# Attention with hash buckets and a mixture of experts on one core: another order for the opening, other gates for the experts' subtractions

## The chip, the cores and the metric

The kernel runs on one core of one Trainium2 chip. The metric is the time of one execution on the device in microseconds (us), the median of several runs. A core has five engines that each run their own list of instructions in order: PE (TensorE, matrix products into PSUM), DVE (VectorE), ACT (ScalarE), POOL (GpSimd) and SP (SyncE, which here only issues transfers). Semaphores order them against each other; 16 DMA engines carry the transfers.

## The reference, cut to what matters

```python
# attention: q, k, v are [4, 8, 768, 64], proj is [64, 6]
q_bits = einsum(q, proj) > 0            # 6 hash bits for each row of q, and of k
mask   = q_bucket[:, None] == k_bucket  # only rows of the same bucket see each other
scores = where(mask, q @ k.T / 8, -1e9)
attn   = exp(scores - max) / (sum + 1e-9)
x      = (attn @ v) as [3072, 512]      # 4 x 768 tokens, 8 heads x 64
# experts: w_gate [512, 8], w1 [8, 512, 1024], w2 [8, 1024, 512], room for 384 tokens each
# greedy choice over the sorted logits x @ w_gate; every token goes to one expert
out[token] = relu(x[token] @ w1[e]) @ w2[e]
```

## The kernel before, in words

**Attention, up to about 425 us.** The 32 heads come in 8 groups of four. For a group the kernel loads q, k and v (`qp`, `kp`, `vp`, 768 KB each, one buffer each) and splits each number into a half-precision part and a remainder: ACT casts (`qh`, `kh`), POOL subtracts (`ql`, `kl`). PE takes the hash bits by a product with `proj`, DVE turns them into signs (`bt`). SP then copies everything into four operands that hold a head's q or k side by side: `qa`, `ka` (rounded parts and hash bits, heads on the second axis) and `qb`, `kb` (rounded parts with the remainders). There are two of each, for odd and even groups (`qa_164` and `qa_168` are the two in the order of before). Group 0 is built piece by piece: heads 0 and 1 straight from loads into `XT`, heads 2 and 3 (its second pair) through `qh`, `kh` and transfers.

A head is worked in 6 steps. In the score pass (`S_pass`, lines 219 and 221) PE forms 128x770 products of `qa` and `ka` and DVE takes their row maxima. In a step (`ST`, lines 243 to 245) PE forms transposed scores, 384 columns at a time, ACT takes the exponential into `pt`; `lo` (line 248, on POOL or DVE) is the remainder of the rounded `pt`; four steps later PE multiplies with `v` (lines 258 to 260). `attention` writes this order out by hand: step t runs `run(2*t)` and `run(2*t+1)`, and the list `at` says what else is emitted at each n = 2t or 2t+1. The table `AP` gives these places: `P1` for group 1's casts, subtractions, hash bits and loads, `MV` for its transfers (`moves`), `OPS` for the whole opening before and during the first steps (one letter an operation: b hash bits of head 0, B those of heads 1 to 3, s score pass, t and r casts into the operands, c and u cast and remainder of the second pair, d and f its transfers, C copies into the other operands' rows 64 to 127, w idle products that keep PE busy). Score passes run up to 9 steps ahead, so that group 1's first one (head 4) stands in PE's list at step 15.

An engine takes its list in order, and SP too: a transfer whose source isn't ready holds up all behind it. Each transfer from SP also waits until the eighth transfer before it has landed.

**Experts, from about 425 us.** `Moe.phase` p chooses the tokens of one expert on DVE with small products on PE (`best`, `compare`, counts, thresholds). `Moe.run` interleaves: while PE works on expert k (`layer1`, 32 pieces, then `layer2`, 36 pieces, 68 in all), the phase of expert k+1 proceeds in steps at the places `E1`, `E2` or `EV`. `wsplit` casts a quarter of a weight on ACT and puts its two subtractions of 128x512 (`wl`, POOL) on a list; `hand(n)` issues n of them right after a step, behind a tiny copy (`tick`) from `s.gate`, so that they start when a chosen instruction of DVE has ended. `HS` says how many follow each step.

Of the kernel before, what the change touches and what calls it, by code (L numbers as in the profile page):

```python
# [33 lines left out]
 MV=[28, 59, 96, 1],  # L34
# [8 lines left out]
def attention(tc, nc, ctx, qT, kT, vv, proj, wg, x_dram, L, jp, identf, B, late=None, after=None):  # L43
# [83 lines left out]
    def bits(G,pairs):  # L127
        if (G,'b') not in TMP: TMP[G,'b']=dp.tile([128,S],F16,name="bt",bufs=1)
        bt=TMP[G,'b']; r=slice(0,128)
        ps=psS.tile([128,2,512],F32,name="pss")  # L130
        for hf in range(2):
            if G==0:
                for w in range(2):
                    T.matmul(ps[32*w:32*w+32,hf,0:384],pr[0:64],(qd,kd)[w][0:64,1,hf*384:hf*384+384],start=True,stop=True,tile_position=(0,32*w))
            for p in pairs:
                for w in range(2):
                    cg=64*p+32*w
                    T.matmul(ps[cg:cg+32,hf,0:384],pr,LD[G][w][:,p,hf*384:hf*384+384],start=True,stop=True,tile_position=(0,cg))
        V.tensor_scalar(bt.rearrange("p (z q) -> p z q",z=2),ps[:,:,0:384],0.0,0.5,op0=ALU.is_gt,op1=ALU.subtract)
        V.tensor_scalar(bt[r],bt[r],8192.0,None,op0=ALU.mult)  # L140
    def dm(G,pairs,eng=SY):
        u=G%2; bt=TMP[G,'b']; h=TMP[G,'h']
        ps=slice(pairs[0],pairs[-1]+1)
        for hh in range(2):
            r=slice(64*hh,64*hh+64); js=slice(2*pairs[0]+hh,2*pairs[-1]+hh+1,2)
            eng.dma_start(QA[u][0:64,js,:],h[0][r,ps]); eng.dma_start(KA[u][0:64,js,0:S],h[1][r,ps])
        for p in pairs:
            for hh in range(2):
                j=2*p+hh
                for w,dst in enumerate((QA,KA)):  # L150
                    a=64*p+32*w+6*hh
                    eng.dma_start(dst[u][64:70,j,0:S],bt[a:a+6,:])
    def dm2(G,pairs):
        u=G%2; h=TMP[G,'h']; l=TMP[G,'l']
        ps=slice(pairs[0],pairs[-1]+1)
        for hh in range(2):
            r=slice(64*hh,64*hh+64); js=slice(2*pairs[0]+hh,2*pairs[-1]+hh+1,2)
            SY.dma_start(QB[u][0:64,js,:],h[0][r,ps]); SY.dma_start(KB[u][64:128,js,:],h[1][r,ps])
            SY.dma_start(KB[u][0:64,js,:],l[1][r,ps]); SY.dma_start(QB[u][64:128,js,:],l[0][r,ps])
    def moves(G):  # L160
# [4 lines left out]
        for r,js in hs: SY.dma_start(QB[u][0:64,js,:],h[0][r])
        if G+1<NG: load(G+1,0)
        for r,js in hs: SY.dma_start(KA[u][0:64,js,0:S],h[1][r])
        for r,js in hs: SY.dma_start(KB[u][64:128,js,:],h[1][r])
        for j in range(4):
            for w,dst in enumerate((QA,KA)):  # L170
                a=64*(j//2)+32*w+6*(j%2)
                SY.dma_start(dst[u][64:70,j,0:S],bt[a:a+6,:])
        if G+1<NG: load(G+1,1)
        for r,js in hs:
            SY.dma_start(KB[u][0:64,js,:],l[1][r]); SY.dma_start(QB[u][64:128,js,:],l[0][r])
# [140 lines left out]
    for G in range(1,NG):  # L316
# [569 lines left out]
```

## Time and profile before

| | us |
|---|---|
| runs | 774.94, 777.45, 779.55 (median 777.45) |
| profiled execution | 781.89 |
| its span in the trace | 780.1 |
| busy: PE, DVE, POOL, ACT | 702.9, 566.8, 550.9, 405.7 |

Times in the rows are from the start of the span. PE is busy for 90% of it, so a gain must come from the remaining stretches in which PE waits, or from those in which its clock is low.

### The profile page before, as it was taken

What the parts mean: (1) busy time and instruction counts of PE and PEld (TensorE: products, weight loads), DVE (VectorE), ACT (ScalarE), POOL (GpSimd) and SP (SyncE); (2) the same over time, 40 slices, a digit from 0 to 9 for tenths busy, and PEclk for the clock granted to TensorE, in tenths of its full rate; (3) what the DMA queues carried; (4) which work ended last, traced back from release to release, by engine and by line L of the source; (5) the groups of instructions that cost most, each with busy time, mean ns of one, the idle gap of its engine ahead of it and who ended that gap; (6) DMA issues with size and microseconds to landing.
All of it is one profiled execution on the core that took longest, in us unless ns stands there. A gap on an engine that the chain in (4) does not pass through costs nothing. (4 is left out here: it accounts for less than half of the span.)

```text
span 780.1 us, 19155 instructions
## 1 busy us (share of the span) xinstructions
PE 702.9 (90%) x7765; PEld 548.6 (70%) x7765; DVE 566.8 (73%) x1321; ACT 405.7 (52%) x790; POOL 550.9 (71%) x481
## 2 busy tenths in 40 slices
PE   8877998999999999998888579989999999999995
PEld 2545665776777767675666478877888887889894
DVE  5866987988888888987765668788887878743120
ACT  6656765677776777755563142524343434334430
POOL 8684749888795978855563366778778787878761
PEclk9998999999999999999998569999999999999998
DMA  7664372715446165320000241625161717162601
GB/s 183 180 146 109 103 188 85 203 63 126 123 117 176 64 151 148 85 74 22 22 22 23 88 169 40 231 74 212 52 244 42 257 42 256 42 229 89 249 28 41
DMA packets 39952, 93.58 MB, mean 120 GB/s; under 512 B 4548, under 2 KB 30520, under 8 KB 37816
## 3 DMA queue, kind: packets, MB, share of 16 engines
q1 hardware_dynamic: 33048, 46.21, 22.5%
q0 software_dynamic: 6816, 46.15, 16.7%
q8 instruction: 61, 1.00, 0.5%
q14 instruction: 27, 0.22, 0.1%
HBM read 59.53 MB, written 12.58 MB: 92 GB/s over the span
## 5 line engine op out<-in xcount | busy, mean ns | idle before, releaser
L248 POOL TENSOR_TENSOR lo<-pt 128x768 f16<-128x768 f32 x143 | 233.7, 1646 | 93.4 <-ACT pt L245 82.2
L245 ACT ACTIVATE pt<-pst 128x384 f32<-128x384 f32 x384 | 182.6, 491 | 97.6 <-PE pst L244 86.7
L221 DVE TENSOR_REDUCE m<-pss 128x1 f16<-128x770 f32 x192 | 182.3, 956 | 50.5 <-PE pss L219 49.6
L243 PE MATMUL pst<-qa,ka 128*128 128x384 f16 x384 | 126.1, 328 | 6.3 <-DVE XT L287 2.8
L244 PE MATMUL pst<-qb,kb 128*128 128x384 f16 x384 | 125.9, 328 | 0.0
L260 PE MATMUL psv<-vh,lo 128*128 128x65 f16 x1152 | 121.0, 194 | 3.5 <-POOL lo L248 3.5
L259 PE MATMUL psv<-vl,pt 128*128 128x64 f16 x1152 | 121.3, 193 | 0.0
L258 PE MATMUL psv<-vh,pt 128*128 128x65 f16 x1152 | 121.3, 194 | 0.0
L258 PEld LDWEIGHTS <-pt 128*128 128x128 bf16 x1152 | 106.7, 98 | 12.8 <-issue 3.3
L219 PE MATMUL pss<-ka,qa 128*128 128x385 f16 x384 | 95.6, 331 | 22.2 <-DVE m L221 12.6
L726 POOL TENSOR_TENSOR wl<-wf,wh 128x512 fp32r<-128x512 f32 x90 | 113.7, 1278 | 0.0
L259 PEld LDWEIGHTS <-pt 128*128 128x128 bf16 x1152 | 105.8, 99 | 9.6 <-issue 0.2
L260 PEld LDWEIGHTS <-lo 128*128 128x128 f16 x1152 | 105.8, 97 | 4.0 <-POOL lo L248 3.9
L716 ACT CAST wh<-wf 128x1024 fp32r<-128x1024 f32 x64 | 66.4, 1048 | 46.5 <-DMA wf<-in_w_dram,zwidx 25.4
L762 ACT ACTIVATE hh<-ph 128x384 fp32r<-128x384 f32 x64 | 31.4, 491 | 88.7 <-PE ph L760 88.6
L219 PEld LDWEIGHTS <-qa 128*128 128x128 f16 x384 | 37.4, 98 | 53.8 <-issue 22.8
L763 DVE SCALAR_TENSOR_TENSOR hl<-ph,hh 128x384 fp32r<-128x384 f32 x64 | 35.2, 554 | 45.6 <-ACT hh L762 45.1
L248 DVE TENSOR_TENSOR lo<-pt 128x768 f16<-128x768 f32 x49 | 62.1, 1268 | 1.5 <-ACT pt L245 1.0
L760 PE MATMUL ph<-xh,wh 128*128 128x384 f32 x256 | 60.9, 351 | 2.2 <-DVE hl L763 1.4
L760 PE MATMUL ph<-xl,wh 128*128 128x384 f32 x256 | 57.4, 343 | 0.0
L760 PE MATMUL ph<-xh,wl 128*128 128x384 f32 x256 | 56.4, 341 | 0.0
L775 ACT COPY o<-po 128x512 f32<-128x512 f32 x24 | 14.1, 587 | 77.1 <-PE po L772 77.1
(261 smaller groups left out, 1435.8 us busy)
## 6 DMA issues: line engine op xcount, KB each, us to landing
vp<-in_vv_dram SPq DMA_DIRECT2D x8, 768.0 KB
x_dram<-X SPq DMA_DIRECT2D x16, 384.0 KB
qp<-in_qT_dram SPq DMA_DIRECT2D x7, 768.0 KB
kp<-in_kT_dram SPq DMA_DIRECT2D x7, 768.0 KB
qa<-qh SPq DMA_DIRECT2D x14, 192.0 KB
qb<-qh SPq DMA_DIRECT2D x14, 192.0 KB
ka<-kh SPq DMA_DIRECT2D x14, 192.0 KB
kb<-kh SPq DMA_DIRECT2D x14, 192.0 KB
```

The lines of the kernel that those rows point to most:

```text
L219: T.matmul(ps[:,hf,0:HK],QA[u][:,j,qc*128:qc*128+128],KA[u][:,j,hf*HK:hf*HK+HK],start=True,stop=True)
L221: V.tensor_reduce(M6[h][:,qc:qc+1],ps[:,:,0:HK],axis=AX.XY,op=ALU.max,negate=True)
L243: T.matmul(ps[:,0:384],KA[u][:,j,kr],QA[u][:,j,r],start=True,stop=False)
L244: T.matmul(ps[:,0:384],KB[u][:,j,kr],QB[u][:,j,r],start=False,stop=True)
L245: A.activation(PT[h,kc][0][:,r],ps[:,0:384],AF.Exp,scale=0.125)
L248: eng.tensor_tensor(l,p,p.bitcast(BF)[:,1::2],op=ALU.subtract)
L258: T.matmul(av[:,c,:],ph[:,r],VH[u][:,j,kc,:],start=(kc==0 and c==0),stop=False,skip_group_check=True)
L259: T.matmul(av[:,c,0:64],ph[:,r],VL[u][:,j,kc,:],start=False,stop=False,skip_group_check=True)
L260: T.matmul(av[:,c,:],l[:,r],VH[u][:,j,kc,:],start=False,stop=False,skip_group_check=True)
L716: s.nc.scalar.copy(h[:,r],f[:,r])
L726: for _ in range(n): s.nc.gpsimd.tensor_tensor(*s.pend.pop(0)[1],op=ALU.subtract)
L760: T.matmul(p[:,0:384],a[:,o:o+128],b[:,d],start=n==0,stop=n==11)
```

## The change

Names and lines: the changed file is 13 lines longer, so line 219 of before is 229 there, 244 is 254, 605 is 618 and so on.

- **Opening.** `tbits` does the bits of q and k of head 0 in one pass, the two products side by side in PE's columns; `prt` (that product's weights) is loaded from ACT's queue in place of POOL's, ahead of everything there. Casts of the constants of head 3 go from ACT to DVE. The hash bits of head 1 and of the second pair are split in `project` (PE) and `signs` (DVE), and three score passes stand ahead of them instead of two. `behind` lets POOL's remainders start only when DVE has written head 0's bits. PE's idle products go from 31 of 384 columns in the opening to 12, and from 5 of 512 to 7.
- **Second pair.** `his` sends all rounded parts (`qa`, `qb`, `ka`, `kb`) as soon as they are cast, then `dbits`, then `lows` (the remainders), then the copies C, and then group 1's loads of q and k.
- **Group 1.** `moves` is cut in three: `qa`, `ka` and the hash bits at n = 23; `qb`, `kb` and group 2's loads at n = 24; the remainders at n = 28. Before, all stood at n = 28, `qb`, `kb` and a load ahead of the bits.
- **Experts.** The gate of the first subtractions of expert 1 is the last `compare`, not the digit before it. In later phases three subtractions follow most threshold steps, none follow the steps of the final chain (lines 602 to 623), two follow the step after; the extra pair at place 46 (`HB`) is gone. Casts of weights stand a little earlier (`W1`, `W2`), result writes one piece later (`SC`). The second quarter of the first weight is subtracted on DVE. `md` loses an accumulator that nothing reads.

In SP's list for the second pair (names: operand <- source; `bt` are hash bits) before:

```order
L146 DMA qa_164<-qh 64x768
L146 DMA ka_165<-kh 64x768
L152 DMA qa_164<-bt 6x768
L152 DMA ka_165<-bt 6x768
L152 DMA qa_164<-bt 6x768
L152 DMA ka_165<-bt 6x768
L58 DMA qp<-in_qT_dram 128x1536
L58 DMA kp<-in_kT_dram 128x1536
L158 DMA qb_166<-qh 64x768
L158 DMA kb_167<-kh 64x768
```

and now:

```order
L158 DMA ka_167<-bt 6x768
L158 DMA qa_166<-bt 6x768
L158 DMA ka_167<-bt 6x768
L161 DMA kb_169<-kl 64x768
L161 DMA qb_168<-ql 64x768
L161 DMA kb_169<-kl 64x768
L161 DMA qb_168<-ql 64x768
L314 DMA qa_170<-qa_166 64x1536 x2
L314 DMA ka_171<-ka_167 64x2x768 x2
L58 DMA qp<-in_qT_dram 128x1536
L58 DMA kp<-in_kT_dram 128x1536
```

The loads `qp`, `kp` stand behind the remainders and the copies (`L314`), where they stood ahead of half of the pair's transfers.

In SP's list for group 1 before:

```order
L164 DMA qa_168<-qh 64x2x768 x2
L165 DMA qb_170<-qh 64x2x768 x2
L58 DMA qp<-in_qT_dram 128x1536
L167 DMA ka_169<-kh 64x2x768 x2
L168 DMA kb_171<-kh 64x2x768 x2
L172 DMA qa_168<-bt 6x768
L172 DMA ka_169<-bt 6x768
L172 DMA qa_168<-bt 6x768
L172 DMA ka_169<-bt 6x768
```

and now:

```order
L168 DMA qa_170<-qh 64x2x768 x2
L168 DMA ka_171<-kh 64x2x768 x2
L173 DMA qa_170<-bt 6x768
L173 DMA ka_171<-bt 6x768
L173 DMA qa_170<-bt 6x768
L173 DMA ka_171<-bt 6x768
L173 DMA qa_170<-bt 6x768
L173 DMA ka_171<-bt 6x768
L173 DMA qa_170<-bt 6x768
L173 DMA ka_171<-bt 6x768
L168 DMA qb_172<-qh 64x2x768 x2
L58 DMA qp<-in_qT_dram 128x1536
```

The bits (`bt`) stand right behind `qa` and `ka`; `qb`, `kb` and the load of the next `qp` went behind them.

In POOL's list for one expert's choice (`ztick<-` names the instruction waited for: `zd` a threshold step, `zsatl`, `zcum` and `zcc` the final chain) before:

```order
L726 TENSOR_TENSOR wl_10568<-wf_10361,wh_10567 128x512 x2
L725 CAST ztick<-zd_10660 1x1
L726 TENSOR_TENSOR wl_10568<-wf_10361,wh_10567 128x512 x2
L781 DMA out_dram<-o,zidx 3072x512
L725 CAST ztick<-zsatl 1x1
L726 TENSOR_TENSOR wl_10568<-wf_10361,wh_10567 128x512 x2
L725 CAST ztick<-zcum 1x1
L726 TENSOR_TENSOR wl_10568<-wf_10361,wh_10567 128x512
L707 DMA wf_10759<-in_w_dram,zwidx 128x4096
L725 CAST ztick<-zcc 1x1
L726 TENSOR_TENSOR wl_10568<-wf_10361,wh_10567 128x512
L699 DMA xg<-x_dram,zidx 128x512 x3
```

and now:

```order
L738 CAST ztick<-zd_10512 1x1
L739 TENSOR_TENSOR wl_10332<-wf_10192,wh_10331 128x512 x2
L794 DMA out_dram<-o,zidx 3072x512
L738 CAST ztick<-zd_10576 1x1
L739 TENSOR_TENSOR wl_10537<-wf_10336,wh_10536 128x512 x3
L738 CAST ztick<-zd_10635 1x1
L739 TENSOR_TENSOR wl_10537<-wf_10336,wh_10536 128x512 x3
L794 DMA out_dram<-o,zidx 3072x512
L720 DMA wf_10727<-in_w_dram,zwidx 128x4096
L738 CAST ztick<-zcc 1x1
L739 TENSOR_TENSOR wl_10537<-wf_10336,wh_10536 128x512 x2
L712 DMA xg<-x_dram,zidx 128x512 x3
```

No subtraction is gated on `zsatl` and `zcum` any more; triples follow `zd`.

The diff, cut to its core:

```diff
- P1=[13, 13, 14, 15, 17, 21, 23, 21, 16, 27, 21, 26, 23, 24, 33, 32, 3, 2, 46, -6, 3, 13],
+ P1=[13, 14, 15, 16, 17, 18, 20, 21, 16, 24, 21, 26, 23, 24, 33, 32, 3, 2, 46, -1, -1, 13],
- MV=[28, 59, 96, 1],
+ MV=[23, 24, 28, 59, 96, 1],
...
+    prt=cp.tile([64,6],F32,name="prt"); A.dma_start(prt,proj)
+    init(3,V.tensor_copy)
...
+    def his(G):
+        u=G%2; h=TMP[G,'h']
+        for qk,(a,b,r0) in enumerate(((QA,QB,0),(KA,KB,64))):
+            for r,j in sides(G): SY.dma_start(a[u][0:64,j,0:S],h[qk][r,1])
+            for r,j in sides(G): SY.dma_start(b[u][r0:r0+64,j,:],h[qk][r,1])
...
+    def lows(G):
+        u=G%2; l=TMP[G,'l']
+        for r,j in sides(G): SY.dma_start(KB[u][0:64,j,:],l[1][r,1]); SY.dma_start(QB[u][64:128,j,:],l[0][r,1])
...
+        if part==1: todo=(go,QA,h[0]),(go,KA,h[1]),(signs_,)
+        elif part==2: todo=(go,QB,h[0]),(nxt,0),(go,KB,h[1],64),(nxt,1)
+        elif part==3: todo=()
+        else: todo=(go,QA,h[0]),(go,QB,h[0]),(nxt,0),(go,KA,h[1]),(go,KB,h[1],64),(signs_,),(nxt,1)
+        for f,*x in todo: f(*x)
+        if part in (0,3): go(KB,l[1]); go(QB,l[0],64)
...
+    def tbits():
+        dst=[a[0][64:70,0,0:S] for a in (QA,KA)]
         for hf in range(2):
             ps=psT.tile([128,512],F32,name="pst"); r=slice(hf*384,hf*384+384)
+            for w in range(2): T.matmul(ps[64+32*w:70+32*w,0:384],prt,(qd,kd)[w][0:64,0,r],start=True,stop=True,tile_position=(0,64+32*w))
...
+    def behind(w):
+        G_.tensor_copy(cp.tile([128,1],F32,name="tick0")[64:65],(QA,KA)[w][0][64:65,0,0:1])
...
-HS=[0,2,2,2,2,2,2,1,1,0]
+HS=[0,3,3,2,3,3,0,0,2,0]
-W2=[3,6,10,16]
+W2=[2,4,7,11]
...
-                s.gate=E[0:1,0,0:1]
+                s.gate=P["OH"][0:1,0,0:1]
+                if ph==1: s.gate=CMP[0][0:1,NC//2-1,0,0:1]
...
-        s.wsplit(0,0,1)
+        s.wsplit(0,0,1,V)
...
-            if p==1: hs[3]=2
+            if p==1: hs=[0,0,0,1,0,2,2,2,2,2,3,0,2,0]
+            if p==2: hs=[0,3,2,2,2,3,2,0,2,0]
-            if p>1: add(b-NS+HB,s.hand,2)
```

## Rows read from the trace of the kernel before

**Rows 1.** The page: TensorE clock granted in 40 slices of the span, in tenths

```profile
PEclk9998999999999999999998569999999999999998
```

**Rows 2.** Table of stretches: us, busy time of each engine, clock, DMA share, GB/s

```profile
35.00:37.00 2.00, 1.02 (x9) 0.69 (x8) 1.97 (x3) 0.00 (x0) 2.00 (x2) 1.00 1.00 238
58.00:59.00 1.00, 0.00 (x0) 0.00 (x0) 0.00 (x0) 0.00 (x0) 0.00 (x0) 0.92 0.34 80
65.00:66.00 1.00, 1.00 (x8) 0.81 (x7) 0.81 (x1) 0.83 (x3) 1.00 (x1) 0.67 0.98 343
```

**Rows 3.** Timeline of PE at step 15 of attention: start us, us, work, [idle before <- releaser]

```profile
61.79 0.80 PE L219 MATMUL pss<-ka,qa 128*128 128x385 f16 x2 [8.26 <-DMA ka<-bt]
```

**Rows 4.** Timeline of SP's queue: start us, us, transfer issued

```profile
28.34 0.38 SPq L58 DMA_DIRECT2D qp<-in_qT_dram  x1
...
45.38 1.29 SPq L164 DMA_DIRECT2D qa<-qh  x2
...
54.27 0.72 SPq L172 DMA_DIRECT2D ka<-bt  x1
```

**Rows 5.** Timeline, opening: start us, us, engine, line, work, [idle before <- releaser]

```profile
5.14 5.28 PE L202 MATMUL pst<-XT,prt 64*6 64x384 f32 x8 [1.62 <-DMA prt<-in_proj_dram]
...
5.82 0.83 ACT L197 CAST ka<-XT 64x768 f16<-64x768 f32 x1
...
10.46 0.56 DVE L203 TENSOR_SCALAR ka<-pst 6x384 f16<-6x384 f32 x1 [0.22 <-PE pst L202]
...
11.05 0.43 DVE L204 TENSOR_SCALAR ka<-ka 6x768 f16<-6x768 f16 x1
...
13.21 0.85 PE L219 MATMUL pss<-ka,qa 128*128 128x385 f16 x2
...
15.23 0.83 PE L134 MATMUL pss<-XT,pr 64*32 64x384 f32 x4
...
26.04 0.32 PE L243 MATMUL pst<-qa,ka 128*128 128x384 f16 x1 [0.57 <-ACT qa L234]
```

**Rows 6.** Timeline of ScalarE in the first round of casts

```profile
37.50 0.93 ACT L124 CAST qh<-qp 128x384 f16<-128x384 f32 x2 [2.91 <-DMA kb<-kl]
```

**Rows 7.** Timeline of VectorE, second group's hash bits

```profile
48.33 0.59 DVE L140 TENSOR_SCALAR bt<-bt 128x768 f16<-128x768 f16 x1
```

**Rows 8.** Stretches of 10 us, columns as in rows 2

```profile
70.00:80.00 10.00, 7.86 (x117) 5.68 (x115) 9.93 (x12) 6.91 (x15) 7.78 (x5) 1.00 0.04 11
...
460.00:470.00 10.00, 8.98 (x42) 8.11 (x43) 6.04 (x29) 4.51 (x11) 6.01 (x6) 0.58 0.01 5
```

**Rows 9.** Timeline of VectorE, second expert's choice

```profile
440.87 1.55 DVE L634 TENSOR_TENSOR ohp<-zmd,iot 128x1536 bf16<-128x1536 bf16 x2
...
455.11 4.26 DVE L486 TENSOR_TENSOR zcmp<-zE,tb 128x1536 bf16<-128x1536 bf16 x2
```

**Rows 10.** Timeline of GpSimd, the same stretch

```profile
449.48 2.51 POOL L719 TENSOR_TENSOR wl<-wf,wh 128x512 fp32r<-128x512 f32 x2
...
455.20 2.48 POOL L726 TENSOR_TENSOR wl<-wf,wh 128x512 fp32r<-128x512 f32 x2
```

**Rows 11.** Timeline of PE, the same stretch

```profile
458.56 0.48 PE L497 MATMUL psa<-zOH,zcmp 128*128 128x8 bf16 x12 [2.76 <-DVE zcmp L486]
```

**Rows 12.** Timeline of GpSimd, a later expert

```profile
558.13 0.18 POOL L725 CAST ztick<-zsatl 1x1 f32<-1x1 bf16 x1
558.28 2.51 POOL L726 TENSOR_TENSOR wl<-wf,wh 128x512 fp32r<-128x512 f32 x2
```

**Rows 13.** Timeline of VectorE, the same later expert

```profile
558.80 2.04 DVE L605 SCALAR_TENSOR_TENSOR zwg<-zd,znn,zmxu 128x24 f32<-128x24 bf16 x1
```

**Rows 14.** Line 605 of VectorE over the run: ns min/median/max

```profile
L605 DVE SCALAR_TENSOR_TENSOR zwg<-zd,znn,zmxu x7: 232/2039/2064, 437.6 to 678.4; 128x24 f32<-128x24 bf16 x7
```

**Rows 15.** Waits of PE, 510 to 580 us, then 580 to 720: us in total, times, longest

```profile
PE psa L626 <- DVE zwidx L691: 3.1, 2, 2.0
...
PE psa L626 <- DVE zwidx L691: 2.2, 2, 1.1
```

More of the change, by code (lines that the diff above doesn't have):

```diff
@@ L127, in bits, with project @@
     def bits(G,pairs):
-        if (G,'b') not in TMP: TMP[G,'b']=dp.tile([128,S],F16,name="bt",bufs=1)
-        bt=TMP[G,'b']; r=slice(0,128)
-        ps=psS.tile([128,2,512],F32,name="pss")
+        project(G,pairs); signs(G)
+    def project(G,pairs):
+        TMP[G,'p']=ps=[psT.tile([128,512],F32,name="pst")[:,None] for _ in range(2)] if G==0 else [psS.tile([128,2,512],F32,name="pss")]
         for hf in range(2):
+            o=ps[hf][:,0] if G==0 else ps[0][:,hf]
             if G==0:
                 for w in range(2):
-                    T.matmul(ps[32*w:32*w+32,hf,0:384],pr[0:64],(qd,kd)[w][0:64,1,hf*384:hf*384+384],start=True,stop=True,tile_position=(0,32*w))
+                    T.matmul(o[32*w:32*w+32,0:384],pr[0:64],(qd,kd)[w][0:64,1,hf*384:hf*384+384],start=True,stop=True,tile_position=(0,32*w))
             for p in pairs:
@@ L137, in bits @@
                     cg=64*p+32*w
[L138 to L143, printed above, removed]
-        for hh in range(2):
[L145 to L160, printed above, removed]
+                    T.matmul(o[cg:cg+32,0:384],pr,LD[G][w][:,p,hf*384:hf*384+384],start=True,stop=True,tile_position=(0,cg))
@@ new lines, in signs, with sides @@
+    def signs(G):
+        bt=TMP[G,'b']=dp.tile([128,S],F16,name="bt",bufs=1); b2=bt.rearrange("p (z q) -> p z q",z=2); z=0
+        for ps in TMP[G,'p']:
+            n=ps.shape[1]; V.tensor_scalar(b2[:,z:z+n],ps[:,:,0:384],0.0,0.5,op0=ALU.is_gt,op1=ALU.subtract); z+=n
+        V.tensor_scalar(bt,bt,8192.0,None,op0=ALU.mult)
+    def sides(G):
+        return [(slice(64*hh,64*hh+64),2+hh) for hh in range(2)]
+    def his(G):
[3 more added lines that the diff above has]
+            for r,j in sides(G): SY.dma_start(b[u][r0:r0+64,j,:],h[qk][r,1])
@@ L162, in moves, with dbits @@
+    def dbits(G):
+        u=G%2; bt=TMP[G,'b']
+        for hh in range(2):
+            for w,dst in enumerate((QA,KA)): SY.dma_start(dst[u][64:70,2+hh,0:S],bt[64+32*w+6*hh:70+32*w+6*hh,:])
+    def lows(G):
+        u=G%2; l=TMP[G,'l']
+        for r,j in sides(G): SY.dma_start(KB[u][0:64,j,:],l[1][r,1]); SY.dma_start(QB[u][64:128,j,:],l[0][r,1])
+    def moves(G,part=0):
         u=G%2; h=TMP[G,'h']; l=TMP[G,'l']; bt=TMP[G,'b']
         hs=[(slice(64*hh,64*hh+64),slice(hh,4,2)) for hh in range(2)]
-        for r,js in hs: SY.dma_start(QA[u][0:64,js,:],h[0][r])
@@ L165, in moves, with go @@
[L165 to L175, printed above, removed]
+        def go(dst,src,r0=0):
+            for r,js in hs: SY.dma_start(dst[u][r0:r0+64,js,0:S],src[r])
@@ new lines, in signs_, with nxt @@
+        def signs_():
+            for j in range(4):
+                for w,dst in enumerate((QA,KA)):
+                    a=64*(j//2)+32*w+6*(j%2)
+                    SY.dma_start(dst[u][64:70,j,0:S],bt[a:a+6,:])
+        def nxt(w):
+            if G+1<NG: load(G+1,w)
+        if part==1: todo=(go,QA,h[0]),(go,KA,h[1]),(signs_,)
+        elif part==2: todo=(go,QB,h[0]),(nxt,0),(go,KB,h[1],64),(nxt,1)
+        elif part==3: todo=()
+        else: todo=(go,QA,h[0]),(go,QB,h[0]),(nxt,0),(go,KA,h[1]),(go,KB,h[1],64),(signs_,),(nxt,1)
@@ L322, in attention @@
         for n in range(4): add(p[8+n],sub,G,n%2,n//2)
-        add(p[12],bits,G,[0,1]); add(AP['MV'][G-1] if G<4 else 48*(G-1)+AP['MV'][3],moves,G)
+        add(p[12],bits,G,[0,1])
+        if G==1:
+            for n in (1,2,3): add(AP['MV'][n-1],moves,G,n)
+        else: add(AP['MV'][G+1] if G<4 else 48*(G-1)+AP['MV'][5],moves,G)
         for j in range(4): add(p[15]+st*j,cv,G,j); add(p[15]+st*j+sg,sv,G,j)
@@ L386 @@
 KW=[1,0,4,0,2,19,7,1]
-SC=15
+SC=16
 class Moe:
@@ L641, in phase @@
         V.tensor_tensor(Gt,pm[:,None,:].to_broadcast([128,4,NC]),s.th,op=ALU.is_ge)
-        V.tensor_scalar(md,mi.bitcast(F32),-4096.0,0.0,op0=ALU.add,op1=ALU.add,accum_out=junk)
+        V.tensor_scalar(md,mi.bitcast(F32),-4096.0,None,op0=ALU.add)
         def left():
```

23 lines of the change are left out of this document (9 added, 14 removed).

## The prediction

> **What bounds the kernel now.** I read the page first. PE is busy for 702.9 of 780.1 us, so 77 us are left in which it waits. The row of granted clocks [rows 1] shows where else time goes: two dips, one in the slices around 60 us and one around 460 us. Then I took the table of stretches at both dips, the waits and the timeline of PE there, and went from each wait to the engine or queue that ended it.
>
> In the opening there are three places. (1) PE's first score pass starts at 13.21, and steps follow one another from 26.04 [rows 5]; until the bits of head 0 are there (DVE's last instruction for them ends at 11.48), PE has only its own fp32 products. (2) ScalarE stands idle for 2.91 us ahead of 37.50, because its casts need group 1's load [rows 6]; PE has 1.02 of 2 us of work at 35 to 37, with the DMA engines full [rows 2]. (3) The largest: PE reaches head 4's score pass at 53.53 and starts it at 61.79, 8.26 us later, released by a transfer of hash bits into `ka` [rows 3]. DVE had finished these bits at 48.92 [rows 7]. The bits lay in SP's order behind `qa`, `qb`, the load `qp`, `ka` and `kb`: the first of these is issued at 45.38, the bits for `ka` at 54.27 [rows 4]. A load is 768 KB and each operand half of that, 2.36 MB in all ahead of the bits. After this idle time PE's clock is low (0.92, then 0.67 at 65 to 66 with PE full) [rows 2].
>
> In the experts, PE waits 2.76 us for expert 1's `compare` [rows 11], and the clock falls with it: 0.58 over 460 to 470 [rows 8]. In later experts it waits at L626 for the end of the choice: 2.0 and 1.1, then twice 1.1 [rows 15], and once more 1.1 put down to another instruction of that chain (L610).
>
> **The change part by part.** Terms are against the profiled run, 781.89 us, which stands 4.44 over the median of 777.45. The span is 780.1; the 1.8 around it stays.
>
> *Head 0's bits.* Eight PE instructions in a row take 5.28 us, two for each of four products, 1.32 a product [rows 5]. Products side by side are seen at L134: two of them, four instructions, in 0.83 us [rows 5]. That row is at full pace, and L219 shows the two paces: 0.85 for its pair at 13.21, about half that once the clock is up. So a pair costs between 0.83 (fast) and 1.66 (slow), and both pairs 1.7 to 3.3 in place of 5.28. With `prt` loaded earlier, PE starts near 5.0 (ScalarE reads head 0's `ka` data from 5.82 without a wait, so the data are there about then) and is done near 8.0. DVE then still has two instructions of 0.56 and two of 0.43 [rows 5], 2.0 in all, so the bits are ready near 9.9 in place of 11.48, and the pass starts there, not at 13.21, as fewer idle products stand ahead of it: 3.3 us earlier. From there to the steps it took 12.83 us; 19 idle products fewer, at the pace of the 0.32 that an overlapping product of the same length shows (0.16 each when they follow closely), are worth 3 of it, of which I count half, 1.4, since DVE's row maxima lie beside them. So the steps begin at 21.3: **4.7** (bounds: 2.1, if the pairs don't run together, and 6.3, with all 3).
>
> *Head 4's bits.* Behind `qa` and `ka` alone they have 0.79 MB ahead of them, not 2.36, and two issues of about 1.3 (1.29 for `qa` [rows 4]). They are ready 4.6 us ahead of PE's arrival (53.53 less 48.92), and all moves together. Two issues of bits, 0.72 for one [rows 4], and a landing of about 2 fit almost into that: I leave 0.5 of the 8.26 (bounds 0 to 3.5, if the landing takes as long as before behind the data). **7.8**. What is late next is `kb`, `qb`, needed a step later, and behind them the remainders at n = 28.
>
> *The clock after it.* With PE idle for 0.5 and not 8, I expect no fall. At the low level, 1.2 in place of 2.4 GHz, PE had about 3.9 us of work from 61.8 to 65.7 (the slice at 65 still shows 0.67 [rows 2]) that takes half as long at the high one: **1.9** (0 to 2.5).
>
> *Casts at 37.* The loads of group 1 now stand last, behind transfers that no longer mix with them; the second pair's rounded parts have gone early. They are issued after the steps' start of 21.3 and that of the transfers ahead, at about 26.5, and I give them half of the 9.2 us from issue to cast that they had (28.34 to 37.50 [rows 4, 6]): there at about 31, at 34 at worst. The casts asked at 34.59 (37.50 less 2.91), some 33 or a little earlier now. PE's **1.0** missing there [rows 2] comes back (0 to 1.0; below nothing in the last rival but one).
>
> *Given back.* PE's idle stretches let DVE and GpSimd catch up. At 70 to 80 DVE is busy 9.93 of 10 us [rows 8]; without the pause its queue is not empty at the start of that. I charge **-1.5**, a sixth of the 9.7 that the two terms before this bring (0 to -4).
>
> *Expert 1's choice.* The two halves of `compare` take 4.26 for the pair [rows 9] while GpSimd runs L726, 2.48 for two [rows 10]. A DVE product of the same shape, with nothing of GpSimd's beside it, takes 1.55 for two [rows 9]. With the gate on the last compare the subtractions start after it: 2.7 us less, and PE's 2.76 [rows 11] is nearly gone, 2.4. At 460 to 470 PE was busy for 8.98 us at 0.58 of the clock [rows 8], work that takes 5.2 at the full one, 3.8 less. The clock fell after a wait as long as this one, but others end in it too: I take half, 1.9. Together **4.3** for expert 1 (1.0 to 6.6). The quarter of the weight that goes to DVE frees 2.51 on GpSimd [rows 10] and costs DVE between the 1.55 of rows 9 and that; DVE is busy 6.04 of 10 us there [rows 8], so nothing.
>
> *Later experts.* L605 works on 128x24 numbers and takes 2.04 us in the middle of seven, 0.23 at best [rows 14]: it starts at 558.80, while GpSimd has two subtractions from 558.28, 2.51 for both, to 560.79, and ends at 560.84 [rows 12, 13]. Nothing is gated on `zsatl` now, so it takes 0.23, 1.8 less; the four waits of 1.1 ([rows 15] and the one at L610) go: **4.4**. Expert 2 keeps its pair there, and its 2.0. The third subtraction behind a threshold step holds the next instruction of DVE that meets it for another 1.25 at most; such steps have slack in three of four, so 0.3 for each of four experts: **-1.2** (0 to -3). The extra pair at place 46 was off the path, as were casts and writes moved by a piece: 0.
>
> *A rule on the third subtraction.* The row: L605, begun in the middle of the first subtraction, came through only when both had ended, 0.05 us after the second [rows 12, 13]. The Trainium skill ("SBUF — State Buffer", "SBUF: two separate sides") says the pair of ports that DVE and GpSimd share is locked for a whole instruction, and the loser blocks for that one. By that alone L605 would have got in after the first subtraction, a third would add nothing, and the sum would be 1.2 better, 755. The trace disagrees here, so I keep the charge.
>
> Sum: 4.7 + 7.8 + 1.9 + 1.0 - 1.5 = 13.9 in the opening; 4.3 + 4.4 - 1.2 = 7.5 in the experts; 21.4 together: 760.5 by the profiled run, and less 4.44, **756**.
>
> **The rivals.** *The opening is bound elsewhere.* When PE no longer waits for bits, DVE (9.93 of 10 [rows 8]) and the transfers (DMA share 1.00 [rows 2]) may bind: 3.5 us of the wait stay, 1.9 of clock with them, and with 12 idle products in place of 31 the clock may come up later, 4 in all at half pace against the row that shows 0.85 for a pair [rows 5]. That loses 9.4: 765. For it: both were full in the rows named. Against: the wait had one cause, and its data were ready.
>
> *The experts give nothing.* Triples cost what the chain gains, as DVE's waits move from L605 to the threshold steps: 781.89 - 13.9 - 4.44 = 763.6, 764. For it: rows 12 and 13 show that a row of subtractions blocks as a whole. Against: threshold steps have PE's work to hide them, the end of the chain has not.
>
> *The other side: the loads placed last.* SP is in order. `qp` and `kp` stand behind the remainders, which need GpSimd, and behind copies that need everything else. With the 9.2 us from issue to cast, and ScalarE asking at about 33, the time counts as follows. The wait of 2.91 cost PE 1.0, so some 1.9 of a wait is free and the rest costs PE as much, since its exponentials stand behind the casts. With about 2 for the clock that falls in so long a wait, all 21.4 are gone when the load lands at 33 + 1.9 + 19.5 = 54.4, so is issued at 45; from there the kernel is slower, and an issue at 50 costs 26: 782. Issues from 41 to 45 leave no difference. For it: one queue, in order. Against: in the order of before all of the second pair had been issued when group 1's `qa` came at 45.38 [rows 4], with time to spare.
>
> *That it doesn't do what it says*: the bits wait on their sources and not on what lies ahead of them. Then the 8.26, and the clock, stay, the -1.5 goes, and the rest counts: 764, a case that I put with the first rival.
>
> **How the numbers follow.** Forecast 756: 0.60; opening bound elsewhere, 765: 0.21; experts nothing, 764: 0.11; loads late, no difference: 0.05, slower: 0.03. The forecast's own bounds don't all fall on one side: the three largest above it (2.6 of the opening, 3.0 of the wait, 3.3 of expert 1) in part reach 762, the better ends (1.6, 0.6, 1.5, 2.3 and 1.2, 7 in all) 749. With the two rivals and some room past them the range is 748 to 768. A measurement of this kernel tells about 0.5%, 3.9 us, from no change. Faster 0.92, same 0.05, slower 0.03.
>
> **What would show it.** In the changed profile: first score pass at about 10 and steps from about 21; no wait over 1 us for `bt` at head 4's pass (L229), and a full clock in the slices after; casts of L125 without a wait for a load; `compare` at about 1.6 for its pair, with PE's wait for it under 0.5; L618 at 0.23 in experts 3 to 6, and no 1.1 at the product behind it. A wait that only moved, a compare still at 4, or threshold compares twice as long as now would make me wrong.

## The result and the profile after

| us | before | changed |
|---|---|---|
| median of the runs | 777.78 (774.94 to 779.55) | 766.21 (764.74 to 767.22) |
| ratio, 95% interval | | 0.9851 [0.9819, 0.9882] |
| profiled execution, span | 781.89, 780.1 | 766.95, 764.9 |

The kernel is 11.6 us faster, about half of the 21.4 that were forecast, and 10 us over the predicted 756. The profiled pair differs by more, 14.9 us. Run again on another chip (E12), the changed kernel was at 771.48, 0.9931 [0.9904, 0.9958] of before: 4.2 us faster, not 11.6. The mean granted clock of each run was lower there, 0.966 to 0.973, where the four runs of this table had 0.975 to 0.977.

The places of the forecast, in their order. The page's row of granted clocks:

```profile
PEclk9999999999999999999997599999999999999999
```

Of the two dips in [rows 1] the one near 60 us is gone; the one where the experts begin stays. PE's timeline at head 4's score pass (the first row) has no idle time in brackets any more, against 8.26 us in [rows 3]:

```profile
49.13 0.49 PE L229 MATMUL pss<-ka,qa 128*128 128x385 f16 x2
49.64 0.49 PE L238 MATMUL pss<-ident,m 128*128 128x128 f16 x6
```

SP's queue says why. The bits for `ka` go out at 45.81, behind `qa` and `ka` alone, and `qb` comes at 50.79; PE asks for them at 49.13, 3.3 us after that issue, and finds them there; in [rows 4] they were issued at 54.27, after PE had asked:

```profile
38.62 1.26 SPq L168 DMA_DIRECT2D qa<-qh  x2
41.85 1.24 SPq L168 DMA_DIRECT2D ka<-kh  x2
...
45.81 0.71 SPq L173 DMA_DIRECT2D ka<-bt  x1
...
50.79 1.38 SPq L168 DMA_DIRECT2D qb<-qh  x2
```

ScalarE's first cast of group 1 still waits, where the forecast had no wait, but for 1.07 us in place of the 2.91 of [rows 6]:

```profile
32.02 0.51 ACT L125 CAST qh<-qp 128x384 f16<-128x384 f32 x1 [1.07 <-DMA qp<-in_qT_dram]
```

PE at the start (compare [rows 5]): head 0's products take 3.56 us in place of 5.28, six idle products follow, and the first score pass starts at 9.75, not 13.21:

```profile
4.32 3.56 PE L209 MATMUL pst<-XT,prt 64*6 64x384 f32 x8
7.81 2.10 PE L73 MATMUL psv<-wrm 128*128 128x384 f16 x6
9.75 1.07 PE L229 MATMUL pss<-ka,qa 128*128 128x385 f16 x4
```

In the experts, VectorE's compare for expert 1 takes 1.82 for its pair, 4.26 before [rows 9] (1.55 in the forecast):

```profile
442.32 1.82 DVE L498 TENSOR_TENSOR zcmp<-zE,tb 128x1536 bf16<-128x1536 bf16 x2
```

So far nearly all is as forecast. But from there the two traces tell another story. I took ScalarE's exponentials of attention (384 in both kernels) and PE's first product `ph` (L773, before L760) of each expert, and set their starts against each other:

| us | before | changed | earlier by |
|---|---|---|---|
| first exponential | 24.0 | 17.4 | 6.7 |
| 33rd (behind head 4's pass) | 64.7 | 51.6 | 13.1 |
| last | 418.1 | 403.9 | 14.2 |
| expert 0's first product | 452.4 | 439.7 | 12.7 |
| expert 1's | 501.1 | 483.9 | 17.2 |
| expert 2's | 543.7 | 528.5 | 15.2 |
| expert 3's | 583.6 | 568.2 | 15.4 |
| expert 6's | 701.7 | 686.1 | 15.6 |
| end of the span | 780.1 | 764.9 | 15.2 |

In this pair the opening brought 14.2 us, where 13.9 were forecast. The experts together brought 1.0, where 7.5 were: 4.5 in the stage of expert 0 (in which expert 1 is chosen), less 1.5 ahead of it and 2.0 in the next; the next four brought 0.4, which the last two lost again.

Two views show what happened there. First expert 2's choice, timeline of all engines:

```profile
500.59 3.35 DVE L623 TENSOR_SCALAR zSTb<-ze,zcm 128x24 bf16<-128x24 f32 x1
...
501.43 2.47 POOL L739 TENSOR_TENSOR wl<-wf,wh 128x512 fp32r<-128x512 f32 x2
...
504.00 0.20 PE L639 MATMUL psa<-zSTb,ntri 128*128 128x48 bf16 x1 [2.69 <-DVE zwidx L704]
```

Expert 2 keeps two subtractions behind `zsatl` (501.43, 2.47 us). Now L623, on 128x24 numbers, sits from 500.59 until they are done, 3.35 us, and PE waits 2.69 for it; before, it waited 2.0 at this place. Second, the digit's own instruction in each threshold step, line 603 (line 590 before; rows of a line's group: engine, count, min/median/max in ns). Before:

```profile
L590 DVE SCALAR_TENSOR_TENSOR zd<-zd,zn,zE x24: 242/244/246, 466.5 to 673.2; 128x24 bf16<-128x24 bf16 x24
L590 DVE SCALAR_TENSOR_TENSOR zd<-zE,psa x6: 248/967/1673, 462.4 to 655.2; 128x24 bf16<-128x24 bf16 x6
```

and now:

```profile
L603 DVE SCALAR_TENSOR_TENSOR zd<-zd,zn,zE x24: 242/591/1768, 450.5 to 657.7; 128x24 bf16<-128x24 bf16 x24
L603 DVE SCALAR_TENSOR_TENSOR zd<-zE,psa x6: 247/248/249, 446.5 to 639.7; 128x24 bf16<-128x24 bf16 x6
```

Before, the 24 of the later steps took 0.24 us each, all of them. Now half take 0.59 or more, and the last one of each of experts 3 to 6 some 1.7. L605's stall of 1.8 has not gone: it is found here. For experts 4 to 6 VectorE's stall was 0.73 (at the first threshold step, 0.97 less 0.24) and 1.81 (L605), 2.5 in all; it is now 0.51, 0.45 and 1.53, 2.5 in all. PE's waits in one such stage were 1.1 (before, 565 to 605); they are now 0.9 (550 to 590):

```profile
PE ph L773 <- DVE hl L776: 0.5, 2, 0.3
PE psa L516 <- DVE zcmp L498: 0.4, 1, 0.4
```

### The profile page after: what moved, and what is told of

Read it like the earlier page. It is cut to its first block, busy times and chain, and to the rows that moved or that the text cites. A ratio compares the mean times of both kernels' runs of the same rounds, so it can differ in the third digit from the quotient of the medians.

```text
span 764.9 us, 19094 instructions
## 1 busy us (share of the span) xinstructions
PE 696.4 (91%) x7748; PEld 544.7 (71%) x7748; DVE 565.7 (74%) x1318; ACT 402.9 (53%) x788; POOL 547.5 (72%) x467
## 3 DMA queue, kind: packets, MB, share of 16 engines
q0 software_dynamic: 6784, 46.14, 17.2%
## 5 line engine op out<-in xcount | busy, mean ns | idle before, releaser
L739 POOL TENSOR_TENSOR wl<-wf,wh 128x512 fp32r<-128x512 f32 x92 | 116.0, 1279 | 0.0
L268 PEld LDWEIGHTS <-pt 128*128 128x128 bf16 x1152 | 106.7, 98 | 12.7 <-issue 3.1
L229 PE MATMUL pss<-ka,qa 128*128 128x385 f16 x384 | 94.3, 328 | 15.5 <-DVE m L231 14.2
L776 DVE SCALAR_TENSOR_TENSOR hl<-ph,hh 128x384 fp32r<-128x384 f32 x64 | 34.8, 555 | 43.3 <-ACT hh L775 42.7
L773 PE MATMUL ph<-xh,wh 128*128 128x384 f32 x256 | 60.7, 352 | 5.7 <-DVE hl L776 3.7
L258 DVE TENSOR_TENSOR lo<-pt 128x768 f16<-128x768 f32 x49 | 61.7, 1258 | 1.5 <-ACT pt L255 1.0
L773 PE MATMUL ph<-xl,wh 128*128 128x384 f32 x256 | 57.4, 343 | 0.0
L773 PE MATMUL ph<-xh,wl 128*128 128x384 f32 x256 | 56.9, 343 | 0.0
```

What stands on the lines that cost most here:

```text
L229: T.matmul(ps[:,hf,0:HK],QA[u][:,j,qc*128:qc*128+128],KA[u][:,j,hf*HK:hf*HK+HK],start=True,stop=True)
L258: eng.tensor_tensor(l,p,p.bitcast(BF)[:,1::2],op=ALU.subtract)
L268: T.matmul(av[:,c,:],ph[:,r],VH[u][:,j,kc,:],start=(kc==0 and c==0),stop=False,skip_group_check=True)
L739: for _ in range(n): s.nc.gpsimd.tensor_tensor(*s.pend.pop(0)[1],op=ALU.subtract)
L773: T.matmul(p[:,0:384],a[:,o:o+128],b[:,d],start=n==0,stop=n==11)
```

## The experiments

Each ran beside the kernel before on the same chip; ratios are to it, with the 95% interval. E1 to E4, E5 to E8 and E9 to E12 each shared a chip. "Stage" is the time from an expert's first product of L773 to the next expert's, so stage 0 is that of expert 0.

**E1 and E2: half of the change each.** E1 joins the new `attention` with the old `Moe` and its tables, E2 the other way round.

> The opening and attention part of the change, with the experts as before. Theory A (the opening brings what was forecast, 13 to 14 us, and the experts about 1): 764 to 767, within 2 us of the changed kernel's 766. Theory B (the experts do bring their 7.5, and the opening brings only 4 over many runs, the profiled pair having been a lucky one): about 773. In the profile both expect head 4's first score pass without a wait for hash bits, and expert 1's compare at over 4 us for its pair again.

> The experts' part of the change, with the opening as before. Theory A: 775 to 778, no difference that can be told; the compare of expert 1 at about 1.8 for its pair, PE's wait for it gone, but expert 2's choice waits some 2.7 us at the end (its pair of subtractions is gated on zsatl) with 3 us of low clock behind it. Theory B: about 770.

E1: 765.45, 0.9815 [0.9756, 0.9874]; E2: 777.83, 0.9987 [0.9957, 1.0018]. The opening is the whole gain that can be told; the experts' part can't be told from nothing (at most some 3 us). In E2's profile the stage 0 is 46.7, in E1's, with the old experts, 45.4. So the 48.7 of the profile before, which had made the new experts look 4.5 better, was a long one of its kind (its clock was low for some 10 us in it, E1's for some 7). The whole experts' part, from the last exponential to the end of the span, says the same: 362.0 before and 361.0 changed, but 359.0 in E1 and in E11, which have the experts of before.

The profile before was a long one at head 4 too. E2 has the same opening, with its bits in the same order, and PE waited 5.28 us there, not 8.26:

```profile
58.77 0.80 PE L219 MATMUL pss<-ka,qa 128*128 128x385 f16 x2 [5.28 <-DMA ka<-bt]
```

E2's 33rd exponential starts at 61.7 and its last one at 414.1, 3.0 and 4.0 ahead of the profile before. Against E2 the changed opening brought 10.2 us, not 14.2.

**E3: expert 2 without the pair behind `zsatl`.**

```diff
-            if p==2: hs=[0,3,2,2,2,3,2,0,2,0]
```

> The changed kernel without the line that gives expert 2 its own places for subtractions: none stands behind zsatl, as in experts 3 to 6. Theory A (that pair costs 2.69 us of PE's waiting and a dip of the clock of 3.4 us behind it): L623 falls from 3.35 to 0.23 us, PE's wait at L639 from 2.69 to under 1, no dip at 505, and 2.5 to 4.5 us less than the changed kernel: 762 to 764. Rival (the pair only moves to another step of the same choice, and the wait with it, as the later experts gained only 0.1 each): within 1 us of 766.

767.27, 0.9831 [0.9771, 0.989]: no gain in the median, which runs on another chip than the changed kernel's. The profile tells more: stage 1 shrank from 44.6 to 42.9, less than the 2.5 to 4.5 of theory A. The timeline of all engines in that choice:

```profile
490.44 3.76 POOL L739 TENSOR_TENSOR wl<-wf,wh 128x512 fp32r<-128x512 f32 x3
...
492.47 1.77 DVE L603 SCALAR_TENSOR_TENSOR zd<-zd,zn,zE 128x24 bf16<-128x24 bf16 x1
...
494.89 0.32 PE L516 MATMUL psa<-zOH,zcmp 128*128 128x32 bf16 x6 [1.39 <-DVE zcmp L498]
```

GpSimd's three subtractions end at 494.20; L603, begun at 492.47, ends at 494.24, and PE stands 1.39 us for the compare behind it. Theory A was right on the place, and the rival on what follows: L639's 2.69 is gone, and this wait came in its stead, with the clock at its lower level for some 3 us behind it.

**E4: group 1's transfers in one piece, in the old order.**

```diff
-            for n in (1,2,3): add(AP['MV'][n-1],moves,G,n)
+            add(AP['MV'][2],moves,G,0)
```

> The changed kernel with group 1's transfers in one piece at n = 28 and in the old order (bits behind qa, qb, the load, ka and kb); the rest of the opening as changed. Theory A: that order alone is what made PE wait at head 4's score pass: a wait of 6 to 9 us comes back at about 49 and a low clock of some 7 us behind it, 8 to 10 us more than the changed kernel: 774 to 776. Rival (the loads and rounded parts sent earlier have cleared the queue, so the order no longer matters): a wait under 3, 766 to 769.

775.19, 0.9961 [0.9933, 0.999]: most of the change's gain is gone, as theory A said; on the same chip E3, whose opening is the changed one, is 7.9 faster. PE's timeline, SP's queue and the stretch behind:

```profile
54.11 0.80 PE L229 MATMUL pss<-ka,qa 128*128 128x385 f16 x2 [4.96 <-DMA qa<-bt]
```

```profile
38.48 1.26 SPq L168 DMA_DIRECT2D qa<-qh  x2
...
47.59 0.76 SPq L173 DMA_DIRECT2D qa<-bt  x1
```

```profile
53.00:60.00 7.00, 5.89 (x39) 4.05 (x40) 2.48 (x3) 3.34 (x6) 2.04 (x2) 0.51 0.57 158
```

The bits are issued from 47.59, behind five larger things as before, PE waits 4.96 us (less than the 6 to 9 of theory A, and about E2's 5.28), and its clock is 0.51 of full over the next 7 us. `qa` goes out at 38.48, no later than the changed kernel's 38.62, so the place n = 28 in the program held nothing up here: what differs is what stands ahead of the bits. Between the first and the 41st exponential E4 loses 7.0 us to the changed kernel; the medians are 9.0 apart.

**E5: pairs behind the thresholds, three and three at the end (experts 2 to 6).**

```diff
-HS=[0,3,3,2,3,3,0,0,2,0]
+HS=[0,2,2,2,2,2,0,0,3,3]
-            if p==2: hs=[0,3,2,2,2,3,2,0,2,0]
```

> The changed kernel with two subtractions behind each threshold step in place of three, none behind zsatl and zcum, and the rest (three and three) behind the last two steps, for experts 2 to 6. Theory C (a step's own instruction at L603 waits until GpSimd has ended its whole row of subtractions, and the 1.8 us that left L618 only moved there): L603 back to 0.24 nearly everywhere, L618 at 0.23 too, PE's waits at L516 and L773 of 0.9 an expert and expert 2's 2.69 with its low clock gone, 4 to 7 us less than the changed kernel in the experts: 760 to 763. Rival (the same GpSimd time must block DVE somewhere: now at the last steps and the next expert's first compare): 764 to 768, with a PE wait of 1 to 2 us an expert at another line.

787.08, 1.0133 [1.0099, 1.0167], slower than before the change and far outside both forecasts. Of theory C the first half held: every L603 took 0.24 or 0.25, every L618 0.23 or 0.24. What it had left out stands in the waits of PE (529 to 574) and in the page's clock row:

```profile
PE po L785 <- POOL wl L840: 1.9, 3, 0.7
PE po L785 <- POOL wl L739: 0.7, 1, 0.7
```

```profile
PEclk9999999999999999999995699989898999999998
```

The remainders of the second weight now come too late for `layer2`. The waits are small, 2.6 us in stage 2, but the clock fell in each of stages 1 to 5, for some 7 us in the first three of them, and stages 2 to 4 took 45.0, 44.8 and 44.4 in place of 39.7. So the third subtraction is there to get GpSimd through its list in time.

**E6 and E12: more idle products, and the changed kernel again.** E6:

```diff
-OPS='i2 b0 t0 w6 r0 r2
+OPS='i2 b0 t0 w14 r0 r2
```

> The changed kernel with 14 in place of 6 idle products of PE ahead of the first score pass. Theory D (in some executions the bits' products run at the full clock, PE then idles 1.3 us ahead of that pass and the clock falls for 6.8 us from 11 to 18, which costs 2 us there and 2 more behind; covering the idle time removes the fall): no fall before 20, median 763 to 765, a spread under 4 us. Rival (the fall has another cause, or the products themselves hold up the pass when the clock is low): the fall stays or the pass comes 1.5 to 2.5 later, 766 to 769.

> The changed kernel once more, beside these three on one chip. Theory D: in some of its executions the clock falls at 11 to 18 us, so it spreads over 5 us, with a median of 765.5 to 768; the kernels with 14 idle products spread less and lie 1 to 2 below it. Rival: no difference between the two in spread or median.

E6: 764.93, 0.9869 [0.9831, 0.9907], the median that theory D had. But its runs go from 764.55 to 772.08, a spread of 7.5 and not under 4. E12: 771.48 (767.0 to 772.91), 0.9931 [0.9904, 0.9958], over theory D's 768; its spread of 5.9 is no wider than the 6.8 and 7.4 of E9 and E11, which have 14 idle products. So the rival holds for the spread. E12's profile is the one to read. PE's timeline and two stretches (busy times, clock, DMA as in [rows 2]):

```profile
4.35 2.33 PE L209 MATMUL pst<-XT,prt 64*6 64x384 f32 x8
6.61 1.15 PE L73 MATMUL psv<-wrm 128*128 128x384 f16 x6
9.08 0.82 PE L229 MATMUL pss<-ka,qa 128*128 128x385 f16 x4 [1.32 <-DVE ka L211]
```

```profile
5.00:10.00 5.00, 3.50 (x17) 1.19 (x17) 3.46 (x8) 3.39 (x5) 2.97 (x13) 1.00 1.02 280
11.00:24.00 13.00, 12.19 (x39) 3.79 (x39) 5.67 (x8) 4.63 (x8) 6.26 (x4) 0.50 0.56 125
```

Here head 0's products run at full pace, 2.33 us. The six idle products end early, PE idles for 1.32 us ahead of the first pass at 9.08, and soon after it its clock is low: 0.50 over 11 to 24. The 33rd exponential starts at 56.3, not at 51.6. In the first profile of the same kernel the products were slow, 3.56, PE went straight on, and the clock stayed up. E6 with fast products:

```profile
4.33 2.35 PE L209 MATMUL pst<-XT,prt 64*6 64x384 f32 x8
6.61 2.45 PE L73 MATMUL psv<-wrm 128*128 128x384 f16 x14
9.08 0.82 PE L229 MATMUL pss<-ka,qa 128*128 128x385 f16 x4
```

Fourteen idle products reach to the pass, and the 33rd exponential is at 50.6. Counted over all profiles with parallel products: with six idle products five of seven show fast products and the 1.32 of idle time, and in four of these five the clock fell (for some 7 us in E1, E3 and E8, twice that in E12; not in E4); with fourteen none of four fell (E6, E9, E10, E11), though only two of these (E6, E10) had fast products. That the idle time is the cause is thus likely, not proved: E4 had it and kept its clock. Nor do the medians prove that covering it pays: E11, which is E1 with 14, is at 0.9876 where E1 is at 0.9815, on another chip and with intervals that overlap.

**E7: head 0's four products one after another**, the loops as before the change.

> The changed kernel with head 0's four bit products one after another, as before the change (the weights still from ScalarE's queue). Forecast: the four take 5.28 us in place of some 3, the first score pass starts about 2 later, and the whole is 1.5 to 2.5 us slower: 768. Rival (the start of the steps is set by DVE's row maxima and PE's clock, not by these products): within 1 us of 766, the 2 us being gone by the first steps.

768.6, 0.9884 [0.9844, 0.9924]. The first row maximum starts at 12.39 (10.53 in the changed kernel's first profile) and the 33rd exponential 2.2 later, as forecast. The medians, 2.4 apart, are on different chips and overlap in their runs. E7's products are slow ones, as those of that first profile are, and its clock holds. Where the products were fast and the clock fell (E1, E3, E8), the 33rd exponential stands at 53.8 to 54.0, no earlier than E7's 53.8: there the parallel products brought nothing.

**E8: expert 1's gate on the digit again.**

```diff
-                if ph==1: s.gate=CMP[0][0:1,NC//2-1,0,0:1]
+                if ph==1: s.gate=E[0:1,0,0:1]
-            if p==1: hs=[0,0,0,1,0,2,2,2,2,2,3,0,2,0]
+            if p==1: hs=[0,0,0,2,0,2,2,2,2,2,2,0,2,0]
```

> The changed kernel with expert 1's first subtractions gated on the digit E again, two of them, beside the compare. Theory: the compare's pair takes over 4 us, PE waits 2.5 to 3 us for it, with a longer low clock behind, 4 to 5 us more than the changed kernel up to the end of expert 1: 770. Rival (the 17.6 of lead after expert 1 came from the other edits, the earlier load and the quarter on DVE): under 1.5 us more.

767.82, 0.9877 [0.9843, 0.9911]. VectorE and PE:

```profile
444.88 4.27 DVE L498 TENSOR_TENSOR zcmp<-zE,tb 128x1536 bf16<-128x1536 bf16 x2
...
448.34 0.49 PE L509 MATMUL psa<-zOH,zcmp 128*128 128x8 bf16 x12 [2.67 <-DVE zcmp L498]
```

The compare is long again and PE waits 2.67 us, yet stage 0 takes 45.4, less than the 46.0 to 46.7 of E2, E3, E4, E6 and E7, which all have the new gate. (The changed kernel's 44.2 is short because its first product came late, after a wait of 2.04 for `xh`; from the last exponential to expert 1's first product it takes 80.1, E8 79.7 and E1 79.5.) The rival was right, though not for its reason. E6's timeline of all engines, with the new gate, shows what PE waits for instead:

```profile
439.23 1.82 DVE L498 TENSOR_TENSOR zcmp<-zE,tb 128x1536 bf16<-128x1536 bf16 x2
...
442.24 1.04 ACT L729 CAST wh<-wf 128x1024 fp32r<-128x1024 f32 x1 [2.84 <-DMA wf<-in_w_dram,zwidx]
443.19 0.48 ACT L775 ACTIVATE hh<-ph 128x384 fp32r<-128x384 f32 x1
...
443.71 0.56 DVE L776 SCALAR_TENSOR_TENSOR hl<-ph,hh 128x384 fp32r<-128x384 f32 x1 [2.66 <-ACT hh L775]
...
444.59 0.16 DVE L591 TENSOR_SCALAR_CACHE_REDUCE zsat<-psa 128x8 bf16<-128x8 f32 x1
...
444.81 0.16 PE L594 MATMUL psa<-zhit,us 128*128 128x1 bf16 x1 [2.59 <-DVE zsat L591]
```

The compare is short, but PE then stands 2.59 us (444.81) for `zsat`. That instruction of VectorE stands behind `hl`, `hl` behind ScalarE's `hh` (443.19), and `hh` behind a cast that has waited 2.84 us for its weight (442.24). This cast is of the first quarter of expert 0's second weight, which PE needs only in `layer2`; it merely stands ahead of `hh` in ScalarE's list (`W2`). It did so before the change too, in ScalarE's timeline there:

```profile
459.55 1.05 ACT L716 CAST wh<-wf 128x1024 fp32r<-128x1024 f32 x1 [4.57 <-DMA wf<-in_w_dram,zwidx]
460.50 0.48 ACT L762 ACTIVATE hh<-ph 128x384 fp32r<-128x384 f32 x1
```

The compare ended at 459.37 there, so behind PE's wait for it this second one lay hidden. Expert 0's weights land no sooner for the compare being short: the cast starts 5.7 us behind the expert's first product in E1 (long compare), 5.6 in E6 (short) and 5.5 in E8 (long). That putting this cast behind `hh` would free the 2.6 us is an argument; no run tried it.

**E9 to E11: what the runs pointed to.** E9 has 14 idle products, E8's gate and, for expert 2,

```diff
-            if p==2: hs=[0,3,2,2,2,3,2,0,2,0]
+            if p==2: hs=[0,2,2,3,3,3,0,0,3,0]
```

E10 adds `HS=[0,3,3,2,2,2,0,0,4,0]` for experts 3 to 6; E11 is E1 with 14 idle products.

> The changed kernel with 14 idle products ahead of the first score pass, expert 1's first pair gated on the digit E again, and expert 2's subtractions spread as 2, 2, 3, 3, 3 behind the threshold steps and 3 behind zcc, none behind zsatl. Theory (expert 1's new gate only moved a wait; expert 2's pair behind zsatl costs 2.7 of waiting and often a dip of the clock): expert 1's stage 45.4 and expert 2's 42.7 or less, together 2.5 under the profile with 14 idle products alone (46.3 and 44.5); median 761 to 763. Rival (what is taken from zsatl blocks a threshold step as in the run with triples): expert 2's stage 43 to 44.5, median 764 to 766.

> The kernel of the run before this one (14 idle products, gate on E, expert 2 as there), and for experts 3 to 6 the places 3, 3, 2, 2, 2 behind the threshold steps, none in the chain, four behind zcc. Theory C: the last threshold step's 1.77 at L603 falls under 0.8 and PE's 0.9 of waits an expert to about 0.5, 0.3 less for each stage (39.4 in place of 39.7): 1 to 1.5 less in all. Rival (GpSimd is then late with the second weight's remainders, as in the run with pairs): PE waits for wl at L785, 1 to 3 us an expert, and the clock falls: 766 to 775.

> The changed opening with 14 idle products, and all the experts as before the change. Theory (the experts' part brings at most 1 us, and costs 2 in expert 2): within 1.5 us of the kernel with the changed experts and 14 idle products, 763 to 766, expert stages of 45.4, 42.7, then 39.9. Rival (the experts' part is worth 2 us or more): 767 or more.

E9: 765.24, 0.9862 [0.9833, 0.9891], below the changed kernel on the same chip by 6.2 us, with intervals that don't touch. Its stages 0 and 1 take 45.5 and 42.6 where E6's take 46.3 and 44.5. The median of 761 to 763 was not reached; 765.24 is the rival's. E9 and E12 differ in three things, so the 6.2 can't be put down to one of them. When the products are slow, fourteen idle ones are too many:

```profile
7.93 3.55 PE L73 MATMUL psv<-wrm 128*128 128x384 f16 x14
11.32 0.82 PE L229 MATMUL pss<-ka,qa 128*128 128x385 f16 x4
```

```profile
11.00:24.00 13.00, 10.44 (x61) 4.58 (x60) 9.89 (x12) 7.59 (x13) 8.05 (x6) 1.00 0.57 125
```

The pass starts at 11.32, 1.6 later than the changed kernel's, but the clock stays at 1.00 from there. E10: 771.48, 0.994 [0.9917, 0.9963]. Its L603 fell from 1.76 to 0.5 as theory C said, and PE then waited for remainders (515 to 600), as the rival said, with stages 2 to 4 of 42.4, 41.1 and 42.5:

```profile
PE po L785 <- POOL wl L739: 3.0, 4, 0.8
```

E11: 766.73, 0.9876 [0.9845, 0.9907], not to be told from E9. With the old experts the changed opening is as good.

## Why the prediction was right, and where it was not

**The number.** The 766 lies in the range of 748 to 768, but not at the forecast: it is the number of the first two rivals, 765 and 764. That it fell inside is in part luck: the same kernel's 771.48 in E12 (with 775.67 for the one before) would have been outside. Of the 10.2 us between 756 and the median, 6.5 are the experts (1.0 in the profiled pair in place of 7.5) and 3.7 the step from the profiled run to the median.

**The last step, "and less 4.44, 756":** the terms were sized on an execution that stands 4.44 over the median, and the 4.44 were then taken off once more. What made that execution long lay, as far as three other profiles show, in stretches that the terms had already counted as gain: 3.0 us of the wait at head 4 (8.26, E2 5.28) and 3.0 in the experts (362.0, E1 and E11 359.0), ahead of expert 1's first product. Without that step the forecast is 760.5. The changed kernel's profile stood only 0.7 over its median.

**Head 4's bits, 7.8, and the clock after it, 1.9:** right in place, and in size against the profile of before. The lead was 4.25 us at the 25th exponential and 13.1 at the 33rd: 8.8 against 9.7. Against E2 it is 4.2 and 10.1, 5.9 in all. E4 shows that the order of the transfers did it.

**Casts at 37, 1.0, and given back, -1.5:** the cast's wait fell by 1.8, and the lead was 13.1 at the 33rd exponential, 12.2 at the least and 14.2 at the last. So nothing was given back for good, and the opening's sum, 14.2 against 13.9, is right in part because errors cancel.

**Head 0's bits, 4.7:** the mechanism was right, the size was that of one execution in which the clock held (the first score pass at 9.75 against 9.9, the lead at the 17th exponential 4.6). The step that failed is "19 idle products fewer ... are worth 3 of it, of which I count half". Taking them away also left PE idle for 1.32 us whenever the products were fast. Where the clock then fell, the 33rd exponential stands at 53.8 to 56.3 in place of 51.6, 2.2 to 4.7 of the gain. The first rival had this, "the clock may come up later", at 4 us.

**Expert 1's choice, 4.3:** failed at "PE's 2.76 is nearly gone, 2.4". The compare fell as forecast, 4.26 to 1.82, but the next thing late was expert 0's second weight by way of ScalarE: PE waited 1.5 to 2.6 us for `zsat` in E2 to E7 (0.3 in the changed kernel's first profile, which had lost 2.04 just before). I never asked when that weight lands, nor what stands behind its cast.

**Later experts, 4.4 and -1.2:** failed at "Nothing is gated on `zsatl` now, so it takes 0.23, 1.8 less". L618 does take 0.23:

```profile
L618 DVE SCALAR_TENSOR_TENSOR zwg<-zd,znn,zmxu x7: 233/234/1640, 423.3 to 664.3; 128x24 f32<-128x24 bf16 x7
```

But the subtractions stall L603 for as long as they had stalled L605 and the first threshold step: 2.5 us an expert before and after. The four stages went from 39.89, 39.86, 39.85 and 38.37 to 39.65, 39.84, 39.76 and 38.34, 0.4 in all, where the two terms had 3.2. The charge of 0.3 for the triples was mis-sized: "such steps have slack in three of four" does not hold for the last step of each expert, where L603 takes 1.7 us and PE then waits 0.4 at L516. That was the second rival, word for word, "as DVE's waits move from L605 to the threshold steps", and the sign named in advance, "a wait that only moved". In E5 and E10, where fewer subtractions stand behind the threshold steps, the row ends too late for `layer2`; that no better place exists is not shown.

**Expert 2, "keeps its pair there, and its 2.0":** it went to 2.69, and in five of the seven profiles with that pair a dip of the clock followed; stage 1 took 44.5 to 44.8 in six of them, 42.7 before. E9's places, without that pair, gave 42.6.

**The rule on blocking.** In [rows 12, 13] L605 had come through only when two subtractions had both ended. E3's row repeats it with three, 494.20 and 494.24. The Trainium skill ("SBUF — State Buffer", "SBUF: two separate sides") says that the one that starts first gets the shared pair of ports for the whole instruction and the other fully blocks. If that is read as one instruction, both rows disagree: VectorE's instruction came through only when the rest of GpSimd's row had ended.

## What to carry to other kernels

When work that stalls another engine is only gated elsewhere, the stall may land there: here 2.5 us an expert did. Where a thinner spread took it off those lines (E5), the work itself came too late. So a forecast has to say where the stall lands before it counts a gain. When a wait is taken away, ask of each engine that the waiting one needs next what it is itself waiting for: here a compare hid a late load. Filling work that looks idle may hold up a clock; before it is cut, find the gap that opens where the work beside it runs faster. And a term that is read from one execution carries that execution's excess: to take the distance from the median off again at the end can count it twice.

## What was not expected of the hardware

The same kernel starts in two ways: head 0's products take 2.3 us in some executions and 3.5 in others. PE's own pace differs: six idle products behind them take 1.15 or 2.10. With the fast start and six idle products PE had 1.32 us of idle time, and in four of five such profiles the clock then fell to its lower level. A wait of PE of 2 us for expert 2 left the clock alone before (stage 1: 42.7); one of 2.7 was followed by a low stretch in five profiles (E2 and E4 among them) but not in E6 and E8.
